# Random-feature attention and a feed-forward in one kernel: feed-forward chunks of 512 tokens with one PSUM bank for h, and float64 weights decoded by VectorE and ScalarE in slices of 1024 columns

## The chip, the cores and the metric

The kernel runs on one core of a Trainium2 chip. The metric is the time on the device in microseconds (us), the median of several runs. TensorE does the matrix products (PE in the profile; PEld is its loading of the stationary operand), VectorE is DVE, ScalarE is ACT, GpSimd is POOL, SyncE is SP and issues the DMAs. Products land in PSUM, which has eight banks of 512 float32 columns on 128 partitions.

## What is computed

Attention with positive random features, then a feed-forward with g(h) = h - tanh(h), on 8 batches of 576 tokens, 8 heads of 64 columns, 128 features, d_model 512 and d_ff 2048:

```python
def phi(x):                      # x: q or k, times 64 ** -0.25
    proj = np.einsum('bhsd,md->bhsm', x, omega)
    h = proj - np.sum(x * x, axis=-1, keepdims=True) / 2.0
    return np.exp(h - np.max(h, axis=-1, keepdims=True)) / np.sqrt(m)
kv = np.einsum('bhsm,bhsd->bhmd', phi(k), v)
num = np.einsum('bhsm,bhmd->bhsd', phi(q), kv)
den = np.einsum('bhsm,bhm->bhs', phi(q), np.sum(phi(k), axis=2))[..., None] + 1e-06
x = (num / den)                  # as [4608 tokens, 512]
h = x @ w_in                     # [4608, 2048]
out = (h - np.tanh(h)) @ w_out   # [4608, 512]
```

q, k, v and omega are float32. The two weight matrices arrive as float64; the kernel gets their 8-byte words.

## The kernel before, in words

**Precision.** A product of float32 operands is made of three fast products: each operand is split into hi (rounded to the format float32r) and lo (the rest), and hi*hi, hi*lo and lo*hi are added up in PSUM. So every operand costs a cast (hi, mostly ScalarE) and a subtraction (lo, mostly VectorE).

**Attention** is cut into units, each a Python generator whose `yield`s separate stages. `k_unit(b, c)` makes kv and the sums z of one batch and one pair of heads; `q_unit(ch, c, ...)` makes 128 rows of x (one pair of heads) for a chunk of 256 tokens: features (L128 to L136, or L146 to L150 in float32), denominators (L322, L325), normalisation (L327 to L331), four transposes into a bank `pt` (L338), the product with kv into a bank `pn` (L346, or L362 and L363), and x. In the "native" mode of the start, units work in float32 directly; later ones use split operands (`k_single`). A unit of queries writes its part of xh and xl itself (L372, L373). `tick` moves every open unit forward by one stage and opens the new ones that a table `start` names for this tick.

**Feed-forward.** Chunks have 256 tokens (TC), 18 in all. For a chunk, a step takes two 128-row slices of d_ff: `ffn_h` (L421) makes h of both side by side in one bank of PSUM, 2 x 12 matmuls of 256 columns, then g = tanh(h) on ScalarE (L432), g = h - g on VectorE (L433), gh (L434, ScalarE) and gl (L435, VectorE or, for the first two chunks, GpSimd). `ffn_out` (L438) adds 12 matmuls of 512 columns to two output banks. The products of a step follow one step after its h. Two banks, h0 and h1, alternate for h. The other banks are po0 and po1 (outputs), pj0 and pj1 (projections), pk, and pt. `ffn_store` (L449) copies an output bank to SBUF and stores it.

**Weights.** `decode` (L384) turns float64 words into hi and lo, 512 or 256 columns at a time: ScalarE scales the upper words (L398), GpSimd scales them back (L399), VectorE shifts, masks and merges them (L400, L402, L405) and multiplies the lower mantissa bits in (L406), ScalarE rounds to hi (L408), GpSimd subtracts (L409), and GpSimd or VectorE adds up lo (L410).

**Order of work.** First batch 0's keys and the queries of chunks 0 and 1 in float32. Then eight steps, in each of which two slices of the weights are decoded and chunks 0 and 1 take their step with them, beside keys of batch 1 and queries of chunks 2 and 3. Then chunk after chunk, with one tick of attention behind each `ffn_h` and each `ffn_out`. The program text is not the order on the chip: `schedule_with_timeline_sim=True` has the tile framework lay out each engine's instructions at build time by its own estimate of when each is ready, with program order as the priority. After that each engine takes its list strictly in order.

Of the kernel before, what the change touches and what calls it, by code (L numbers as in the profile page):

```python
# [22 lines left out]
NS = NF // 2          # steps of the feed-forward: two slices each  # L23
# [8 lines left out]
def favor_attention_ffn(ctx: ExitStack, tc: tile.TileContext, qT, kT, va, vb, vt, omT, w_in, w_out, out):  # L32
# [12 lines left out]
    # SBUF: from the left the constants, the working tiles and the weights, as they are decoded;  # L45
    # from the right the tiles of the attention and the scratch of the decoding.
# [12 lines left out]
    # What differs between the start and the rest: buffers, PSUM banks and engines.  # L59
# [26 lines left out]
    omf = sb.tile([P, DM], F32, tag="o", name="omf")[:, 0:M]  # L86
# [5 lines left out]
    ones = const.tile([P, P], F32R, name="ones")  # L92
    nc.scalar.activation(ones, ident, AF.Copy, bias=1.0, scale=0.0)
    om2 = om.rearrange("p a m -> p (a m)")
    aq = open_pool("aq")
    kv0 = open_pool("kv0")
    # both heads' at once for tokens in float32, with -SCALE
    om_bd = kv0.tile([P, 2, M], F32, name="om_bd")
# [24 lines left out]
        # om hi and om lo side by side in one pass, added on the way out  # L123
# [15 lines left out]
    def features_f(f, toks, name):  # L139
        """The same for tokens of both heads as float32 in one pass: [tile, head]."""  # L140
# [12 lines left out]
    kvf = {}   # batch: [kv | 0] and [0 | kv] of each head pair, in float32  # L153
    kvs = {}   # (batch, head pair): [kv hi | lo] of both heads, z on every partition

    def k_unit(b, c):
        """kv and z of the heads 2c and 2c + 1 of batch b, a stage at a time."""
        n = f"{b}_{c}"
        f = att("kf", [P, S], F32, f"kf_{n}")
        nc.sync.dma_start(f, kT[c, :, b * S : (b + 1) * S])  # L160
# [4 lines left out]
        nc.sync.dma_start(v[:, 0:4, 0:D], va[b, c, 0])  # L165
        nc.sync.dma_start(v[:, 6:10, 0:D], va[b, c, 1])
        nc.sync.dma_start(v[0:D, 4:6, 0:D], vb[b, c])
# [16 lines left out]
        # head 0 as columns [hi | lo], head 1 as [lo | hi]  # L184
# [17 lines left out]
    def k_single(b, c, f):  # L202
        """The same by single-pass products: [v hi | v lo]^T [k hi | k lo], whose four parts add up
        to kv^T. z is ones^T times the sum of the tiles of k."""
        n = f"{b}_{c}"
        v = att("vr", [P, 9, D], F32, f"v_{n}")
        nc.sync.dma_start(v, vt[b - 2, c])
        yield
# [5 lines left out]
        pk = ps.tile([P, 2, 2, M], F32, tag=bank("pk"), name=f"pk_{n}")  # L214
        zs = att("zs", [P, 2, M], F32, f"zs_{n}")

        def split(ph, t, n_t):
            """k and v of n_t tiles from t on as [hi | lo], by pairs."""
            ku = []
            for g in range(0, n_t, 2):  # L220
# [7 lines left out]
                else:   # the tile of both heads, kept apart by zeros  # L228
# [22 lines left out]
        ku = split(pa, 0, 4)  # L251
        zsum(pa, 0)
        yield
        pm = features(tiles[4:5], f"km{n}")
        kv(0, ku, True, False)
# [22 lines left out]
        for i in range(2):  # L278
            nc.tensor.matmul(pk[:, 1].rearrange("p h m -> p (h m)"), ones,  # L279
                             zhl[:, i].rearrange("p h m -> p (h m)"), start=i == 0, stop=i == 1)  # L280
        kvt = att("kvs", [P, 2, D], F32, f"kvs_{n}")
# [9 lines left out]
    def q_unit(ch, c, x_out):  # L291
        """The rows of x of the heads 2c and 2c + 1 for chunk ch, a stage at a time."""
        n = f"{ch}_{c}"
        t0 = ch * TC
        pieces = []   # of the chunk, by batch
        t = t0
        while t < t0 + TC:
            e = min((t // S + 1) * S, t0 + TC)
            pieces.append((t // S, t - t0, e - t0))
            t = e  # L300
        f = att("qf", [P, TC], F32, f"qf_{n}")
        native = mode["native"]
        nc.sync.dma_start(f, qT[c, :, t0 : t0 + TC])
# [4 lines left out]
        else:  # L308
            x = att("qx", [P, 2, TC], F32R, f"qx_{n}")
# [26 lines left out]
        pt = ps.tile([P, 2 * TC], F32, tag=bank("pt"), name=f"pt_{n}")  # L336
        for i in range(4):
            nc.tensor.transpose(pt[:, i * P : (i + 1) * P], ph[:, ix(i // 2, i % 2)], ident)  # L338
        if native and all(b in kvf for b, s, e in pieces):
            qf = att("qh", [P, 2, TC], F32, f"qt_{n}")  # L340
            nc.scalar.copy(qf.rearrange("p h t -> p (h t)"), pt)
            yield
            pn = ps.tile([P, TC], F32, tag=bank("pt"), name=f"pn_{n}")
# [8 lines left out]
        qh = att("qh", [P, 2, TC], F32R, f"qh_{n}")  # L352
        ql = att("ql", [P, 2, TC], F32R, f"ql_{n}")
# [4 lines left out]
        pn = ps.tile([P, 2, TC], F32, tag=bank("pt"), name=f"pn_{n}")  # L358
# [5 lines left out]
        tmp = att("tmp", [P, TC], F32, f"tmp_{n}")  # L364
        xs = sb.tile([P, TC], F32, tag="xs", name=f"xs_{n}", bufs=2)
# [4 lines left out]
        yield  # L370
        xh, xl = x_out(ch)
        nc.scalar.copy(xh[:, c], xs)  # L372
        mode["lo"].tensor_sub(xl[:, c], xs, xh[:, c].bitcast(F32))  # L373
        xdone[ch] = xdone.get(ch, 0) + 1

# [181 lines left out]
    while gens:  # L557
        tick()
# [81 lines left out]
```

## Time and profile before

| | |
|---|---|
| median of 3 runs | 1107.13 us (1106.38 to 1108.35) |
| profiled execution, first to last instruction | 1105.4 us |
| instructions | 21115 |
| mean granted TensorE clock | 0.986 |
| DMA | 55.94 MB, mean 51 GB/s |

In the profile, a row of a group gives line, engine, operation, the tiles written and read, the shape and count; then total busy time and the mean duration in ns; then the idle time of the engine just before, with what ended it. A row of the timeline gives start and duration in us from the span's start. PEclk is the share of its full clock that TensorE was granted. Matmuls are pipelined, so their durations overlap and only the distance of their starts is a price.

### The profile page before, as it was taken

To read this page: it belongs to the slowest core of one execution; us is meant where nothing else is said; L and a number is where in the kernel's file an instruction comes from. 1 tells how busy PE (TensorE), PEld (TensorE's weight loads), DVE (VectorE), ACT (ScalarE), POOL (GpSimd) and SP (SyncE) were. 2 spreads that over 40 slices of the span, in tenths; PEclk is the share of its full clock that TensorE was granted. 3 is DMA by queue.
4 is the path that set the end of the run, shared out by engine and by line. 5 is a ranking of instruction groups with operands and counts; after the bars stand their busy time and mean duration, and the time that the engine had idled before them with its cause. 6 is when DMAs were issued, how large, how long until landed. Compare 5 with 4: busy or idle time off the path is not lost. (4 is left out here: it accounts for less than half of the span.)

```text
span 1105.4 us, 21115 instructions
## 1 busy us (share of the span) xinstructions
PE 1063.0 (96%) x6968; PEld 966.1 (87%) x6968; DVE 900.0 (81%) x3079; ACT 703.7 (64%) x1850; POOL 403.1 (36%) x659
## 2 busy tenths in 40 slices
PE   9797888799999999999999999999999999999998
PEld 7577677689989999999999999899999999999997
DVE  5989999989999888678888888998888888666522
ACT  6654445577677776567776776677777766556421
POOL 2787677635553331023333333343333333000000
PEclk9989889999999999999999999999999999999999
DMA  8233312221111111101111111111111110000000
GB/s 232 95 117 99 117 65 96 65 69 31 60 32 51 32 51 32 34 11 51 32 51 29 51 32 51 32 52 32 52 32 51 32 36 15 30 10 25 1 20 20
DMA packets 39244, 55.94 MB, mean 51 GB/s; under 512 B 12896, under 2 KB 22240, under 8 KB 39136
## 3 DMA queue, kind: packets, MB, share of 16 engines
q1 hardware_dynamic: 39056, 54.57, 15.9%
q8 instruction: 55, 0.90, 0.3%
q14 instruction: 53, 0.43, 0.1%
q10 hardware_dynamic: 80, 0.03, 0.0%
HBM read 45.15 MB, written 9.44 MB: 49 GB/s over the span
## 5 line engine op out<-in xcount | busy, mean ns | idle before, releaser
L428 PE MATMUL h<-xh,wih 128*128 128x256 f32 x1152 | 331.0, 288 | 7.7 <-DVE g L433 7.5
L428 PE MATMUL h<-xh,wil 128*128 128x256 f32 x1152 | 329.9, 287 | 2.2 <-DVE wil L410 1.9
L428 PE MATMUL h<-xl,wih 128*128 128x256 f32 x1152 | 329.9, 286 | 0.0
L428 PEld LDWEIGHTS h<-xh,wih 128*128 128x128 f32 x1152 | 221.0, 192 | 14.9 <-issue 5.5
L428 PEld LDWEIGHTS h<-xl,wih 128*128 128x128 f32 x1152 | 221.3, 192 | 4.6 <-issue 0.8
L428 PEld LDWEIGHTS h<-xh,wil 128*128 128x128 f32 x1152 | 221.2, 192 | 3.5 <-DVE wil L410 2.4
L445 PE MATMUL po<-woh,gh 128*128 128x512 f32 x544 | 214.2, 394 | 0.0
L446 PE MATMUL po<-wol,gh 128*128 128x512 f32 x544 | 214.0, 393 | 0.0
L447 PE MATMUL po<-woh,gl 128*128 128x512 f32 x544 | 211.9, 391 | 0.0
L433 DVE TENSOR_TENSOR g<-h,g 128x512 f32<-128x512 f32 x144 | 98.8, 686 | 59.8 <-ACT g L432 58.9
L434 ACT CAST gh<-g 128x512 fp32r<-128x512 f32 x144 | 89.4, 621 | 86.0 <-DVE g L433 83.0
L432 ACT ACTIVATE g<-h 128x512 f32<-128x512 f32 x144 | 85.2, 592 | 87.6 <-PE h L428 79.2
L435 DVE TENSOR_TENSOR gl<-g,gh 128x512 fp32r<-128x512 f32 x128 | 99.7, 779 | 37.8 <-ACT gh L434 36.2
L447 PEld LDWEIGHTS po<-woh,gl 128*128 128x128 f32 x544 | 102.3, 188 | 21.0 <-DVE gl L435 0.4
L445 PEld LDWEIGHTS po<-woh,gh 128*128 128x128 f32 x544 | 102.7, 189 | 16.2
L446 PEld LDWEIGHTS po<-wol,gh 128*128 128x128 f32 x544 | 102.7, 189 | 14.9
L322 DVE CUSTOM_DVE_ANT_0 junk<-phi_q,zb 128x128 f32<-128x128 f32 (+1 forms) x320 | 101.8, 321 | 13.8 <-ACT zb L285 0.4
L225 POOL TENSOR_TENSOR khl<-phi_ka,khl 128x256 fp32r<-128x256 f32 x48 | 38.2, 801 | 116.9 <-DVE khl L224 109.8
L136 ACT ACTIVATE phi_q<-phi_q,nb_q 128x128 f32<-128x128 f32 x232 | 75.7, 391 | 2.5 <-DVE nb_q L132 2.2
L233 POOL CAST vhl<-v 128x128 fp32r<-128x128 f32 (+1 forms) x144 | 45.2, 315 | 85.2 <-PE pk L241 73.8
L356 DVE TENSOR_TENSOR ql<-pt,qh 128x512 fp32r<-128x512 f32 x64 | 43.9, 686 | 29.6 <-ACT qh L355 29.3
L338 PE MATMUL pt<-ident,phi_q 128*128 128x128 f32 x288 | 50.0, 279 | 11.2 <-DVE xs L369 3.8
(152 smaller groups left out, 2198.6 us busy)
## 6 DMA issues: line engine op xcount, KB each, us to landing
kf<-kT SPq DMA_DIRECT2D x32, 288.0 KB, 2.9
qf<-qT SPq DMA_DIRECT2D x72, 128.0 KB, 2.1
out<-o SPq DMA_DIRECT2D x36, 256.0 KB, 2.0
v<-vt SPq DMA_DIRECT2D x24, 288.0 KB, 2.8
raw_i<-w_in SPq DMA_DIRECT2D x12, 512.0 KB, 3.9
raw_o<-w_out SPq DMA_DIRECT2D x12, 512.0 KB, 3.3
v<-va SPq DMA_DIRECT2D x16, 128.0 KB, 3.6
raw_i<-w_in SPq DMA_DIRECT2D x8, 256.0 KB, 2.8
```

Of the source, the lines that this page charges most:

```text
L136: nc.scalar.activation(ph[:, j], ph[:, j], AF.Exp, bias=nb[:, j : j + 1], scale=-1.0)
L233: nc.gpsimd.tensor_copy(u[p, i, 0], v[p, j])
L322: nc.vector.tensor_tensor_reduce(bank("junk")[r], ph[r, i], kvs[b, c][1][r, h], scale=1.0, scalar=EPS, op0=ALU.mult, op1=ALU.add, accum_ou ...
L338: nc.tensor.transpose(pt[:, i * P : (i + 1) * P], ph[:, ix(i // 2, i % 2)], ident)
L428: nc.tensor.matmul(p[:, j], w, x, start=i == 0, stop=i == len(prods) - 1)
L432: nc.scalar.activation(g, p, AF.Tanh)
L433: nc.vector.tensor_sub(g, p, g)
L434: nc.scalar.copy(gh, g)
L435: mode["gl"].tensor_sub(gl, g, gh.bitcast(F32))
L445: nc.tensor.matmul(po[t], h, woh[f], start=first, stop=False)
L446: nc.tensor.matmul(po[t], h, wol[f], start=False, stop=False)
L447: nc.tensor.matmul(po[t], l, woh[f], start=False, stop=last)
```

## The change

- `TC` becomes 512, with 9 chunks; units of queries keep 256 tokens (`TQ`). A step of the feed-forward is one slice of d_ff: 12 matmuls of 512 columns for h, 12 for the outputs.
- h has a single bank, `h`. Four banks hold the outputs (po0 to po3), one is pk, and two, a0 and a1, take turns for projections, transposes and `pn`.
- x is written as float32 by the query units and split for a whole chunk by `split_x`, into single buffers. Finished outputs are copied into those x tiles, by ScalarE and VectorE in turn, and stored from there.
- In `ffn_out` the products with gl come after all others of the step, except in the last slice.
- A slice of w_in and one of w_out lie together, 1024 columns, fetched by one DMA (`fetch`) and decoded by nine passes, three on ScalarE and six on VectorE; GpSimd has none. There are two raw buffers and one each of the working tiles a and m.
- The weights are decoded beside one first chunk (512 tokens), a slice per step, with the keys of batch 1, half of batch 2's, and the queries of the next 512 tokens, all in float32. In this phase the loads of SyncE's queue are kept in program order (`load`).
- Of the first eight units' normalisations VectorE takes half; in the first chunk ScalarE takes all. gl is always VectorE's.

```diff
-TC = 256              # tokens of a chunk
+TC = 512
+TQ = 256
+NW0 = 10
...
+    def load(dst, src):
+        i = nc.sync.dma_start(dst, src)
+        if mode.get("chain"):
+            tc.keep_in_program_order(i)
...
-            xh, xl = x_out(ch)
-            nc.scalar.copy(xh[:, c], pn)
-            nc.vector.tensor_sub(xl[:, c], pn, xh[:, c].bitcast(F32))
+            nc.scalar.copy(x_out(ch, c), pn)
...
+    def fetch(f):
+        raws[f] = dec.tile([P, 2 * DM], U64, tag="raw", name=f"raw{f}", bufs=2)
+        load(raws[f], w[f])
...
+    def decode(f):
...
+        a = dec.tile([P, 2 * DM], U32, tag="a", name=f"a{f}", bufs=1)
+        m = dec.tile([P, 2 * DM], U32, tag="m", name=f"m{f}", bufs=1)
+        p = raws[f].bitcast(U32)[:, 0 : 2 * DM]
+        nc.scalar.activation(m, mid, AF.Copy, scale=128.0)
+        nc.scalar.activation(a.bitcast(F32), topf, AF.Abs)
+        nc.vector.tensor_scalar(a.bitcast(F32), a.bitcast(F32), 2.0**-15, 122879.9921875,
+                                op0=ALU.max, op1=ALU.min)
+        nc.vector.tensor_scalar(a, a, 3, 0x3FFFF000, op0=ALU.logical_shift_left, op1=ALU.bitwise_and)
+        nc.vector.scalar_tensor_tensor(out=a, in0=top, scalar=0xC0000000, in1=a,
                                        op0=ALU.bitwise_and, op1=ALU.bitwise_or)
+        nc.scalar.copy(hi, a.bitcast(F32))
+        nc.vector.scalar_tensor_tensor(out=m, in0=top, scalar=23, in1=m,
+                                       op0=ALU.logical_shift_left, op1=ALU.bitwise_or)
+        nc.vector.tensor_scalar(p, a, 0xFF800000, None, op0=ALU.bitwise_and)
+        nc.vector.scalar_tensor_tensor(out=lo, in0=m, scalar=2.0**-43, in1=p.bitcast(F32),
                                        op0=ALU.mult, op1=ALU.mult)
...
+    def split_x(n):
+        xhs[n] = []
+        for c in range(NC):
+            xh, xl = [sb.tile([P, TC], F32R, tag=f"x{k}{c}", name=f"x{k}{c}_{n}") for k in "hl"]
+            nc.scalar.copy(xh, xfs[n][c])
+            nc.vector.tensor_sub(xl, xfs[n][c], xh.bitcast(F32))
+            xhs[n].append((xh, xl))
...
+    def ffn_h(n, s):
+        p = ps.tile([P, TC], F32, tag="h", name=f"h_{n}_{s}")
+        prods = [(wt[s][:, i, c * P : (c + 1) * P], xhs[n][c][j]) for c in range(NC)
+                 for i, j in ((0, 0), (0, 1), (1, 0))]
...
+    def run(n, s):
+        prev = state["prev"]
+        def beat():
+            tick(start.pop(state["t"], ()))
+            state["t"] += 1
+        def h():
+            if s == 0:
+                while sum(xdone.get(n * TC // TQ + i, 0) for i in range(TC // TQ)) < NC * TC // TQ:
+                    tick((), True)
+                split_x(n)
+            state["prev"] = (n, s, *ffn_h(n, s))
+        h()
+        beat()
+        if prev is not None:
+            ffn_out(*prev)
+            if s == 0:
+                ffn_store(n - 1)
+        beat()
...
+    ab = ["a0", "a1"]
+    mode.update(pj=ab, pk=["pk"], pt=ab, norm=[nc.scalar], kvw=(sb, 6), zb=(sb, 6))
...
+    for s in range(NF):
+        if len(wt) == NW0 and not start and not gens:
             close_pool("a0")
+            weight_tiles(open_pool("w1", "left"), range(NW0, NF))
+        decode(s)
+        if fetched < NF:
+            fetch(fetched)
+            fetched += 1
+        run(0, s)
```

More of the change, by code (lines that the diff above doesn't have):

```diff
@@ L369, in q_unit @@
         nc.vector.tensor_add(xs[D:P], pn[D:P, 1], tmp[D:P])
[L370 to L373, printed above, removed]
         xdone[ch] = xdone.get(ch, 0) + 1
-    wih, wil, woh, wol = {}, {}, {}, {}
+    wt = {}
     def weight_tiles(pool, fs):
         for f in fs:
-            for name, d in (("wih", wih), ("wil", wil), ("woh", woh), ("wol", wol)):
-                d[f] = pool.tile([P, DM], F32R, name=f"{name}{f}")
@@ L412, in decode_slice @@
[L412 to L431 removed]
+            wt[f] = pool.tile([P, 2, 2 * DM], F32R, name=f"w{f}")
@@ L434, in ffn_h @@
         nc.scalar.copy(gh, g)
-        mode["gl"].tensor_sub(gl, g, gh.bitcast(F32))
+        nc.vector.tensor_sub(gl, g, gh.bitcast(F32))
         return gh, gl
-    def ffn_out(s, gh, gl, po):
-        for t in range(TC // P):
-            for j in range(2):
-                f = 2 * s + j
-                h = gh[:, j, t * P : (t + 1) * P]
-                l = gl[:, j, t * P : (t + 1) * P]
-                first, last = f == 0, f == NF - 1
-                nc.tensor.matmul(po[t], h, woh[f], start=first, stop=False)
-                nc.tensor.matmul(po[t], h, wol[f], start=False, stop=False)
-                nc.tensor.matmul(po[t], l, woh[f], start=False, stop=last)
@@ L463, in out_tiles, with ffn_out @@
-    def out_tiles(ch, tags=("po0", "po1")):
-        return [ps.tile([P, DM], F32, tag=t, name=f"{t}_{ch}") for t in tags]
-    need = {b: (b * S) // TC for b in range(B)}
-    x_of = {}
+    po = {}
+    def ffn_out(n, s, gh, gl):
+        if s == 0:
+            po[n] = [ps.tile([P, DM], F32, tag=f"po{t}", name=f"po{t}_{n}") for t in range(TC // P)]
+        first, last = s == 0, s == NF - 1
+        tok = [slice(t * P, (t + 1) * P) for t in range(TC // P)]
+        for t, p in enumerate(po[n]):
+            nc.tensor.matmul(p, gh[:, tok[t]], wt[s][:, 0, DM:], start=first, stop=False)
+            nc.tensor.matmul(p, gh[:, tok[t]], wt[s][:, 1, DM:], start=False, stop=False)
+            if last:
+                nc.tensor.matmul(p, gl[:, tok[t]], wt[s][:, 0, DM:], start=False, stop=True)
+        if not last:
+            for t, p in enumerate(po[n]):
+                nc.tensor.matmul(p, gl[:, tok[t]], wt[s][:, 0, DM:], start=False, stop=False)
@@ new lines, in ffn_store @@
+    def ffn_store(n):
+        for t, p in enumerate(po[n]):
+            o = xfs[min(n + 1, NCH - 1)][t]
+            r = n * TC + t * P
+            if n == NCH - 1 and t == TC // P - 1:
+                for e, h in ((nc.vector, slice(0, DM // 2)), (nc.scalar, slice(DM // 2, DM))):
+                    copy(e, o[:, h], p[:, h])
+                    nc.sync.dma_start(out[r : r + P, h], o[:, h])
+            else:
+                copy((nc.scalar, nc.vector)[t % 2], o, p)
+                nc.sync.dma_start(out[r : r + P, :], o)
@@ L469, in favor_attention_ffn @@
+    need = {b: (b * S) // TQ for b in range(B)}
+    xfs, xhs = {}, {}
     xdone = {}
@@ L601, in favor_attention_ffn @@
-    ffn_out(*prev)
-    ffn_store(NCH - 1, prev[-1])
+            start.setdefault(16 * (need[b] - 4) - 17 + 6 * c, []).append(("k", b, c))
+    start = {t0 + k: v for k, v in start.items()}
+    for n in range(1, NCH):
+        for s in range(NF):
+            run(n, s)
+    ffn_out(*state["prev"])
+    ffn_store(NCH - 1)
     for name in list(pools)[::-1]:
```

265 lines of the change are left out of this document (85 added, 180 removed).

## The prediction

> **What bounds the kernel now.** I read the page's first part, then the busy time by stretch, then single matmuls in the timeline.
>
> ```profile
> PE 1063.0 (96%) x6968; PEld 966.1 (87%) x6968; DVE 900.0 (81%) x3079; ACT 703.7 (64%) x1850; POOL 403.1 (36%) x659
> ```
>
> ```profile
> core 0 of [0], span 1105.4 us
> core 0: us, PE busy (x) PEld busy (x) DVE busy (x) ACT busy (x) POOL busy (x), PEclk, DMA share, GB/s
> 0.00:215.00 215.00, 178.76 (x980) 149.68 (x980) 193.71 (x399) 115.34 (x304) 147.70 (x175) 0.93 0.35 111
> 215.00:400.00 185.00, 183.15 (x1245) 168.55 (x1246) 166.34 (x618) 136.18 (x363) 80.32 (x147) 1.00 0.16 48
> 400.00:1000.00 600.00, 599.38 (x4093) 555.43 (x4092) 496.62 (x1941) 413.73 (x1103) 175.08 (x338) 1.00 0.12 36
> 1000.00:1105.00 105.00, 101.66 (x654) 92.40 (x653) 43.32 (x124) 38.47 (x82) 0.00 (x0) 1.00 0.04 16
> ```
>
> The reader should see two kernels in one. From 215 us on TensorE has work at all times (599.38 of 600 us), so there only cheaper matmuls, or waits put between them, move the end. In the first 215 us TensorE lacks 36 us and runs at 0.93 of its clock, while VectorE is 90% busy: there the decoding of the weights sets the pace. The change touches both.
>
> **Part 1: 512 tokens per matmul of h.** Counts are from the code: h has 18 chunks x 16 slices x 12 = 3456 matmuls of 256 columns now, and 9 x 16 x 12 = 1728 of 512 afterwards. The products for the output stay 1728 of 512. Near the end no attention is mixed in, and the pitch can be read off:
>
> ```profile
> 1051.05 0.40 PE L445 MATMUL po<-woh,gh 128*128 128x512 f32 x1
> ...
> 1053.80 0.28 PE L428 MATMUL h<-xh,wih 128*128 128x256 f32 x1
> ...
> 1056.67 0.40 PE L445 MATMUL po<-woh,gh 128*128 128x512 f32 x1
> ```
>
> Twelve matmuls of 512 columns lie between the first two rows: 2.75 us, 0.229 us each. Twenty-four of 256 lie between the second and third: 2.87 us, 0.1196 us each. (The durations in the rows are longer because matmuls overlap; only starts count.) Today's cost of h is 3456 x 0.1196 = 413.3 us; at the pitch of the output products it becomes 1728 x 0.229 = 395.7 us. Unrounded pitches keep it at 17 to 19 us; I take **-18 us**. Bounds: nothing, if two 256s simply add up to a 512 for these operands (the output products have the activations stationary, h has the weights); on the other side -19, since no row shows a shorter pitch at this width. The nearest row is the same shape on the same engine, so I stay with it.
>
> The Trainium skill (TensorE: Matmul & The Clock Gate, "Wait — 56ns, not 53.3ns?") gives a warm matmul N/2.4 GHz plus about 2.5 ns; this speaks against the gain. By that rule the 1728 matmuls saved are worth an estimated 4 us, not 18. The trace disagrees with the rule in both pitches (119.6 and 229 ns against 109 and 216), so I go by the rows.
>
> **Part 2: the decoding.** Everything VectorE does for it today writes or reads a_i or a_o:
>
> ```profile
> 0.00:215.00 215.00, 61.57 (x84) 11.81 (x20) 34.54 (x36) 0.93 0.35 111
> ```
>
> ```profile
> 0.00:215.00 215.00, 78.09 (x96) 11.62 (x20) 17.73 (x24) 0.93 0.35 111
> ```
>
> The columns are VectorE, ScalarE, GpSimd; VectorE spends 61.57 + 78.09 = 139.7 us. The same operations have very different durations in it:
>
> ```profile
> L402 DVE SCALAR_TENSOR_TENSOR raw_o<-raw_o,a_o x8: 674/1026/1792, 44.6 to 122.1; 128x512 uint32<-128x512 uint32 x8
> ```
>
> ```profile
> L402 DVE SCALAR_TENSOR_TENSOR raw_o<-raw_o,a_o x6: 409/421/430, 178.9 to 211.7; 128x256 uint32<-128x256 uint32 x6
> ```
>
> ```profile
> L400 DVE TENSOR_SCALAR a_i<-a_i x9: 413/1505/1516, 30.9 to 120.6; 128x512 uint32<-128x512 uint32 x9
> ```
>
> ```profile
> L400 DVE TENSOR_SCALAR a_i<-a_i x4: 264/340/527, 186.8 to 203.0; 128x256 uint32<-128x256 uint32 x4
> ```
>
> The figures are minimum/median/maximum in ns. An instruction costs 674 ns undisturbed and up to 1792 with GpSimd at work beside it (147.70 us busy in this stretch). The change takes GpSimd out of the decoding, so I price by minima, extended to 1024 columns: two-input operations 674 + 2 x (674 - 409) = 1204 ns, one-input operations 413 + 2 x (413 - 264) = 711 ns. A slice has three of each: 5.75 us, 16 slices **92 us** (upper bound: today's 139.7). ScalarE gets three passes per slice:
>
> ```profile
> L398 ACT ACTIVATE a_i<-raw_i x9: 662/669/750, 41.2 to 125.9; 128x512 f32<-128x512 f32 x9
> ```
>
> ```profile
> L398 ACT ACTIVATE a_i<-raw_i x4: 429/437/448, 182.6 to 198.4; 128x256 f32<-128x256 f32 x4
> ```
>
> That is 669 + 2 x (669 - 437) = 1133 ns, 54 us in all. Today there are two passes, 11.81 + 11.62 us for one and about as much for the other, so ScalarE gains some 8 us of work; at 115.34 of 215 us busy it has room.
>
> VectorE takes over the residue gl of the first slices, which GpSimd makes now:
>
> ```profile
> L433 DVE TENSOR_TENSOR g<-h,g 128x512 f32<-128x512 f32 x144 | 98.8, 686 | 59.8 <-ACT g L432 58.9
> ...
> L435 DVE TENSOR_TENSOR gl<-g,gh 128x512 fp32r<-128x512 f32 x128 | 99.7, 779 | 37.8 <-ACT gh L434 36.2
> ```
>
> Of 144 residues 128 are VectorE's, so 16 more at about 0.69: 11 us. Half of the 32 normalisations of the first eight query units move to it, at the price it pays later:
>
> ```profile
> L331 DVE TENSOR_SCALAR phi_q<-phi_q,dn 128x128 f32<-128x128 f32 x177 | 47.8, 325 | 1.0
> ```
>
> 16 x 0.325 = 5 us. The start also has more attention in it. Up to 215 us there are now these, one reduction per query unit and three per key unit:
>
> ```profile
> L148 DVE TENSOR_REDUCE nb_k<-pj_k 128x4 f32<-128x512 f32 (+1 forms) x24 | 14.1, 592 | 6.0 <-PE pj_k L146 6.0
> ...
> L148 DVE TENSOR_REDUCE nb_q<-pj_q 128x4 f32<-128x512 f32 x13 | 8.8, 681 | 0.9 <-PE pj_q L146 0.9
> ```
>
> That is 13 query and 8 key units; by the new order of work 16 and 10 are started before the first 512 tokens end. VectorE's attention so far is 193.71 - 139.7 - 10 (g) = 44 us for 21 units, 2.1 each: 5 more are 10.5 us. So VectorE has 193.7 - 139.7 + 92 + 11 + 5 + 10.5 = 172.5 us to do before the first 512 tokens are through; today that point is here, where the first output is copied out:
>
> ```profile
> 220.76 0.58 ACT L456 COPY o<-po 128x512 f32<-128x512 f32 x1
> ```
>
> At today's 90% share 172.5 us take 192 us, at 80% they take 216. I take 85%, 203 us: the start stays short of work as before, and the single buffers of a and m tie ScalarE's pass for slice f+1 to VectorE's last operation of slice f (with ScalarE's pass of 1.1 us exposed on all 16 slices that wait would cost 18 us; other VectorE work covers it). This is 18 us earlier. The five extra units are also off TensorE's later list: about 16 matmuls for a query unit, 23 for a key unit, 3 x 16 + 2 x 23 = 94 at 0.12 us: 11 us. **-29 us** in all; by the two shares -40 and -16, and nothing at all if the share falls to 74%.
>
> The loads stand in SyncE's queue in program order now, so a fetch whose buffer is not free holds back the key and query loads behind it. A slice's 1 MB needs at most two of these:
>
> ```profile
> raw_i<-w_in SPq DMA_DIRECT2D x12, 512.0 KB, 3.9
> ```
>
> 7.8 us against over 10 us per slice on VectorE: hidden, by a buffer that is fetched one slice ahead. If decoding fell under 8 us, this would be next.
>
> **Part 3: what the banks cost.** Four banks go to the outputs, so h has one instead of two: the matmuls of slice s+1 must wait for the tanh and the subtraction of slice s, and TensorE's whole queue stands behind them. Between two blocks of h lie 12 output products (2.75 us) and attention. The trace shows how late the subtraction comes when nothing forces it; these are the first and last cases from 244 us on in which it ends after the next block has begun:
>
> ```profile
> 247.10 0.68 DVE L433 TENSOR_TENSOR g<-h,g 128x512 f32<-128x512 f32 x1
> 247.11 0.28 PE L428 MATMUL h<-xh,wih 128*128 128x256 f32 x1
> ```
>
> ```profile
> 1063.12 0.69 DVE L433 TENSOR_TENSOR g<-h,g 128x512 f32<-128x512 f32 x1 [3.03 <-ACT g L432]
> ...
> 1063.68 0.28 PE L428 MATMUL h<-xh,wih 128*128 128x256 f32 x1
> ```
>
> There are 39 such steps of 124, and they are late by 61 us together. That is the upper bound. But the order on each engine is planned anew: attention matmuls, now mostly inside the block of h, can be moved into the gap. How many there are:
>
> ```profile
> L433 DVE TENSOR_TENSOR g<-h,g 128x512 f32<-128x512 f32 x86 | 59.0, 686 | 18.5 <-ACT g L432 17.9
> ```
>
> This row is for 400 to 1000 us: 600 / 86 = 6.97 us per step, less 5.62 us of feed-forward, 1.35 us of attention. With these the gap is 4.0 us, and only 16 of 124 steps end later than that, by 11 us together. That is the lower bound; I take **+16 us**, nearer to it, because a held TensorE also gives VectorE (83% busy there) time to catch up.
>
> At each of the 8 changes of chunk the four x tiles are split anew, into single buffers, only after the last h of the old chunk: four casts and four subtractions of about 0.7 us. The first pair lets the first three matmuls go, and 2.75 us of output products lie before them, as many more (the last slice's) can be taken forward: 0 to 2 us each, **+5 us**. The projections and transposes share two banks instead of three, and the finished outputs leave from the x tiles. I put both at nothing: TensorE has other matmuls to take while an attention step waits; without that cover each late evacuation would hold it by about 1 us. The end has the same copy and store, halved between two engines: under 0.5 us.
>
> **Sum.** Against the profiled span: 1105.4 - 18 - 29 + 16 + 5 = 1079.4 us. The median of the runs, 1107.13, lies 1.7 us above this span, so **1081 us**.
>
> **The rivals.** *The bank of h becomes the bound (slower).* In the 112 steps with attention beside them the subtraction queues behind attention on VectorE as it does now, and TensorE stands still. For: the 39 late steps, and a VectorE that grows busier. Against: the new order above, and that TensorE now waits for g no longer than this, 7.5 us in 1152 first matmuls of a triple:
>
> ```profile
> L428 PE MATMUL h<-xh,wih 128*128 128x256 f32 x1152 | 331.0, 288 | 7.7 <-DVE g L433 7.5
> ```
>
>  With the full 61 us and 10 us at the chunk changes: 1107.1 - 18 - 29 + 61 + 10 = 1131 us. It decides from 42 us of waits, 0.37 us per step.
>
> *The start gains nothing.* VectorE stays at 74% because decode, attention and feed-forward hand each other work through ScalarE. Then 1107.1 - 18 + 16 + 5 = 1110 us.
>
> *The wider matmul is no cheaper.* Two 256s make one 512 in h: 1081 + 18 = 1099 us. The rule of the Trainium skill in Part 1 would give an estimated 1095.
>
> **How the numbers follow.** Forecast 0.52 (own range 1060 to 1099: the start's two shares, with 11 and 0 us of waits in Part 3, or 16 and 10), h bank 0.21, start 0.13, pitch 0.09, the rest for mixtures. Within 0.2% is about 2.2 us, what a measurement of this kernel can tell from no change. Faster: 0.52 + 0.09, the better part of the start's case and of the mixtures: 0.69; same 0.05; slower 0.26. For 8 in 10 the range reaches from 1060 to 1118: it takes in the other two cases and the bank's up to 48 us of waits.
>
> **What would show it.** Right: starts of h matmuls 0.229 us apart; VectorE instructions of the decode near 0.71 and 1.2 us; the first output copied out near 203 us; waits of h for g of about 16 us in the waits view; a stretch from 400 to 900 us in which TensorE still has work 97% of the time. Wrong: idle TensorE before the first matmul of each h, over 0.37 us on the mean; a first output after 215 us; a pitch near 0.239.

## The result, and the profile after

The changed kernel takes 1337.32 us (median of 4 runs, 1332.91 to 1341.42) against 1107.37 us (4 runs, 1106.38 to 1108.35): a ratio of 1.2077, 95% interval 1.2048 to 1.2105. The forecast was 1081 us and the range ended at 1118. The profiled execution is 1334.4 us long, at a mean granted clock of 0.878 instead of 0.986.

From the page, the busy times and two of its strips of 40 slices (33 us each):

```profile
PE 1170.8 (88%) x5258; PEld 937.7 (70%) x5258; DVE 871.0 (65%) x2925; ACT 725.6 (54%) x1769; POOL 242.8 (18%) x472
...
PE   9699877999789976998699976998699967997898
...
PEclk9799978899869985999589956998589966997799
```

Every engine's share fell, so none of them became the bound: something makes all of them wait, and the strips show a dip about every 4.3 slices, which is the time of one chunk. TensorE's clock dips with its work. Of the 229 us between the two spans, TensorE's idle time makes up 121 (163.6 us instead of 42.4); the other 108 are busy time, although the matmuls were to become cheaper. The busy time by stretch, in the order start, second chunk, one chunk change, the rest of that chunk's attention, end:

```profile
core 0: us, PE busy (x) PEld busy (x) DVE busy (x) ACT busy (x) POOL busy (x), PEclk, DMA share, GB/s
0.00:241.00 241.00, 202.59 (x920) 156.65 (x920) 179.13 (x409) 154.04 (x359) 23.46 (x34) 0.91 0.35 108
241.00:346.00 105.00, 104.59 (x505) 87.83 (x506) 70.48 (x257) 59.17 (x144) 21.82 (x41) 0.97 0.11 31
776.00:818.00 42.00, 25.10 (x81) 17.95 (x81) 29.30 (x129) 24.05 (x66) 9.90 (x20) 0.50 0.14 43
829.00:914.00 85.00, 85.00 (x421) 71.66 (x420) 58.28 (x200) 47.31 (x118) 23.73 (x50) 1.00 0.07 20
1210.00:1334.00 124.00, 105.44 (x433) 82.66 (x431) 40.97 (x105) 35.12 (x71) 0.00 (x0) 0.89 0.05 19
```

Inside a chunk TensorE is full (85.00 of 85 us). At the change of chunk it does 81 matmuls in 42 us, at half its clock. TensorE's timeline at that change, with the first row of each group of three h matmuls and the waits in brackets (idle time before, and what ended it):

```profile
776.34 0.63 PE L435 MATMUL h<-xh,w 128*128 128x512 f32 x1
...
788.88 0.77 PE L136 MATMUL pj_q<-om,qx 128*128 128x256 f32 x2 [0.92 <-DVE x L375]
789.44 0.79 PE L435 MATMUL h<-xh,w 128*128 128x512 f32 x1
...
794.35 1.12 PE L346 MATMUL pt<-ident,phi_q 128*128 128x128 f32 x4 [1.95 <-DVE phi_q L339]
...
806.10 0.77 PE L136 MATMUL pj_q<-om,qx 128*128 128x256 f32 x2 [3.50 <-DVE x L375]
806.66 0.79 PE L435 MATMUL h<-xh,w 128*128 128x512 f32 x1
...
810.79 1.08 PE L346 MATMUL pt<-ident,phi_q 128*128 128x128 f32 x4 [2.20 <-DVE phi_q L339]
...
817.48 0.79 PE L435 MATMUL h<-xh,w 128*128 128x512 f32 x1
```

The 12 matmuls of the chunk's first h need four x tiles, and the last query units of the chunk, one for each tile, are still on their way. They come one behind the other: the projections (pj_q) of a unit wait until L375 has read the `pn` of the unit before out of the bank, then its transposes wait for its normalisation, and only after its x come the next three matmuls of h. What should have been 2.75 us takes 41 us. With the clock at a half, an h matmul lasts 0.63 to 0.80 us there, instead of 0.39 inside the chunk; how much of the 108 us the clock makes up was not separated.

Where the 229 us between the two spans come from, by the starts of the first h matmul of each chunk of 512 tokens (for the kernel before, of each second chunk):

| | before | after | difference |
|---|---|---|---|
| start, up to the second 512 tokens | 216.3 us | 241.4 us | +25 |
| each of the next seven times 512 tokens, mean | 112.5 us | 138.4 us | 7 x 25.9 = +181 |
| last 512 tokens, to the end | 101.6 us | 123.9 us | +22 |

### The profile page after: what moved, and what is told of

Read it like the earlier page. It is cut to its first block, busy times and chain, and to the rows that moved or that the text cites. A ratio compares the mean times of both kernels' runs of the same rounds, so it can differ in the third digit from the quotient of the medians.

```text
span 1334.4 us, 17184 instructions
## 1 busy us (share of the span) xinstructions
PE 1170.8 (88%) x5258; PEld 937.7 (70%) x5258; DVE 871.0 (65%) x2925; ACT 725.6 (54%) x1769; POOL 242.8 (18%) x472
## 4 chain that ended last, share of the span: by engine, by line
PE 70%; DVE 14%; ACT 9%; issue 3%; DMA 2%; POOL 1%; SPq 0%; DVEq 0%; ACTq 0%; POOLq 0%
PE h L435 29%; PE po L453 9%; PE po L454 9%; PE po L459 8%; PE pt L346 3%; PE pn L369 2%; DVE junk L330 2%; PE pk L247 2%; PE pj_q L136 2%; PE pn L368 2%; DMA raw<-w 1%; DVE ql L362 1%; PE pk L187 1%; PE pj_k L154 1%; DVE x L375 1%
## 5 line engine op out<-in xcount | busy, mean ns | idle before, releaser
L435 PE MATMUL h<-xh,w 128*128 128x512 f32 x1152 | 419.4, 422 | 24.5 <-DVE g L440 17.2
L435 PEld LDWEIGHTS h<-xh,w 128*128 128x128 f32 x1152 | 231.5, 201 | 77.4 <-DVE g L440 20.8
L435 PE MATMUL h<-xl,w 128*128 128x512 f32 x576 | 242.4, 421 | 0.4 <-DVE xl L427 0.2
L453 PE MATMUL po<-w,gh 128*128 128x512 f32 x576 | 227.7, 395 | 2.1 <-ACT gh L441 2.1
L454 PE MATMUL po<-w,gh 128*128 128x512 f32 x576 | 226.1, 393 | 0.0
L459 PE MATMUL po<-w,gl 128*128 128x512 f32 x540 | 156.7, 394 | 0.0
L435 PEld LDWEIGHTS h<-xl,w 128*128 128x128 f32 x576 | 116.0, 201 | 30.0 <-DVE xl L427 9.8
L453 PEld LDWEIGHTS po<-w,gh 128*128 128x128 f32 x576 | 109.3, 190 | 25.2 <-ACT gh L441 3.0
L454 PEld LDWEIGHTS po<-w,gh 128*128 128x128 f32 x576 | 109.1, 189 | 21.1
L459 PEld LDWEIGHTS po<-w,gl 128*128 128x128 f32 x540 | 96.8, 188 | 16.5 <-DVE raw L416 0.4
L136 PE MATMUL pj_q<-om,qx 128*128 128x256 f32 x224 | 56.6, 341 | 32.9 <-DVE x L375 31.4
L136 PEld LDWEIGHTS pj_q<-om,qx 128*128 128x128 f32 x224 | 44.8, 229 | 42.8 <-ACT phi_q L137 17.1
```

The source lines that it names most:

```text
L136: nc.tensor.matmul(pj[:, i], lhs[g + i], om2, start=True, stop=True)
L435: nc.tensor.matmul(p, w_, x, start=i == 0, stop=i == len(prods) - 1)
L453: nc.tensor.matmul(p, gh[:, tok[t]], wt[s][:, 0, DM:], start=first, stop=False)
L454: nc.tensor.matmul(p, gh[:, tok[t]], wt[s][:, 1, DM:], start=False, stop=False)
L459: nc.tensor.matmul(p, gl[:, tok[t]], wt[s][:, 0, DM:], start=False, stop=False)
```

## The experiments

Four theories stood against each other. **T1**: projections, transposes and `pn` share two banks in fixed turn, in place of three, so query units pass one behind the other, the feed-forward runs ahead of them and stands at the chunk change. **T2**: the single bank of h. **T3**: the single SBUF buffers of the units (qf, qx, tmp) make their chain long. **T4**: in the start, loads kept in program order delay the weights. "Order" is the variant of T1 in which TensorE's list, not the banks, does the harm.

A third bank cannot simply be given to the changed kernel, whose eight banks are all in use. In the first two runs, and in all later ones of the changed kernel with a third bank, the outputs of the third and fourth token tile are therefore summed in one bank: their separation is left out, the number of matmuls is not changed. Each time below is from a single run unless a ratio stands with it; the four runs of the changed kernel lie 8.5 us apart.

**A third bank for attention** (the bank freed takes pt and pn from the second chunk on):

```diff
-        po[n] = [ps.tile(..., tag=f"po{t}") for t in range(TC // P)]
+        po[n] = [ps.tile(..., tag=f"po{t}") for t in range(TC // P - 1)]
+        po[n].append(po[n][-1])
...
+        pj=["a0", "a1"], pt=["po3"],
```

> The products of the last two token tiles of a chunk go to one output bank (so these two tiles' outputs are not kept apart and the output is not the reference's; the number and shape of all matmuls stay), and the bank set free serves the transposes and kv products of the query units from the second chunk on, beside the two banks of the projections, as before the change. Theory 1, the attention's units go one after another because projections, transposes and kv products share two banks in turn: the distance of query units beside the feed-forward falls from 20 to 26 us to about 14 us, the waits of 30 to 43 us at each change of chunk fall under 5 us, and the time falls from 1337 to about 1130 us (1090 to 1170). Theory 2, the single bank of h holds TensorE: no change, above 1310 us. Theory 3, the units are slow by their single buffers in SBUF or by their own chain beside wide matmuls: above 1290 us.

Measured: 1159.66 us, clock 0.960, so 178 us less, of which 90 are idle time of TensorE and 87 busy time. The total came as expected, the chunk changes did not: from the third to the eighth chunk the twelve matmuls of the first h, 2.5 us long in the last chunk, still lie over 8 to 18 us (31 to 42 with two banks), and the waits were to fall under 5. The buffers were not touched, so T3 alone does not explain the 178 us. The kernel before, from its third chunk on, also has one buffer each of qx, qh, ql and tmp, and two of qf. It has two of each split x tile, the changed kernel one; more buffers were not run.

**The same bank for h instead.**

```diff
+        tag="h" if s % 2 == 0 or n == 0 else "po3"
```

> The same bank is set free in the same way (outputs of the last two token tiles not kept apart), but it is given to h as a second bank, in turn with the first, from the second chunk on. Theory 2, the single bank of h holds TensorE: the time falls to 1200 us or less. Theories 1 and 3: within 25 us of 1337 us, with the same waits of 30 to 43 us at the changes of chunk.

Measured: 1339.73 us. T2 falls. The outputs share a bank here too, so that was not what helped in the run before.

**Two banks, but one for each kind.**

```diff
+        pj=["a0"], pt=["a1"],
```

> From the second chunk on projections have bank a0 to themselves and transposes and kv products bank a1; no bank is added. Theory 1: the next unit's projections no longer wait for the x of the unit before, but two pairs of tiles now share one projection bank; the time falls to 1180 to 1270 us. Theories 2 and 3: within 25 us of 1337 us, or slower.

Measured: 1316.07 us, 21 less. T1 had expected far more: the fixed turn, one half of that theory, is not the main harm.

**Loads free of program order.**

```diff
-        chain=True, kvw=(a0, 4),
+        chain=False, kvw=(a0, 4),
```

> The loads of the first chunk are no longer kept in program order, all else as after the change. Theory 4, the fetches of the weights stand behind key and query loads whose buffers are not free: the fetches of slices 7 to 12, now up to 29 us apart, come 10 us apart or less, the last slice is decoded by about 205 us instead of 234, and the time falls by 20 to 35 us to about 1308 us. If VectorE's own work sets the pace of the decoding: the last slice is decoded at 225 us or later and the time stays within 10 us of 1337.

Measured: 1330.57 us, a miss in size: 7 us, no more than runs of the changed kernel differ by, of which 5 are in the start (the second chunk begins at 236 us). The last slice is decoded at 227 us, as for the rival, but not by its cause (see "The start").

The pace of attention can be counted. L375 (L369 in the kernel before) runs once for each query unit; these are its rows between 400 and 1000 us, of the kernel before, after, and after with a third bank:

```profile
L369 DVE TENSOR_TENSOR xs<-pn,tmp x44: 427/428/430, 403.9 to 999.5; 64x256 f32<-64x256 f32 x44
```

```profile
L375 DVE TENSOR_TENSOR x<-pn,tmp x33: 427/428/429, 412.4 to 985.8; 64x256 f32<-64x256 f32 x33
```

```profile
L375 DVE TENSOR_TENSOR x<-pn,tmp x42: 427/427/429, 403.6 to 999.1; 64x256 f32<-64x256 f32 x42
```

44 units in 596 us before, one per 13.9 us; 33 in 573 us after, one per 17.9; 42 with the third bank, one per 14.5. Since every 512 tokens take eight units, their pace and the time of a chunk are one and the same; that the banks set it is shown by the runs that change the banks alone. TensorE's waits in the two versions of the changed kernel (total, times, longest), first with two banks, then with three:

```profile
PE pj_q L136 <- DVE x L375: 31.4, 19, 3.8
PE pt L346 <- DVE phi_q L339: 28.7, 22, 2.9
PE h L435 <- DVE g L440: 17.2, 9, 4.9
```

```profile
PE h L435 <- DVE g L440: 16.1, 8, 4.9
PE pt L346 <- ACT phi_q L337: 5.2, 5, 2.9
```

Both of the units' waits go with the third bank (pt for phi_q of VectorE falls to 1.8 us; the 5.2 us for ScalarE's were 5.1 with two banks), and that of h for g, the bank I had feared, is nearly the same.

**Order or banks.** In the changed kernel, at the changes to its sixth, seventh and eighth chunk, about 102 of a chunk's some 203 attention matmuls stand in TensorE's list between the start of the last step of one chunk and the start of the second step of the next: half of them in two of sixteen steps. In the kernel before it is mostly 18 to 34 of some 95, about what two of eight steps would hold if they were spread evenly. So the next runs keep TensorE's list in program order, in which it is 16 to 23 of some 200 at most changes, on two banks and on three:

```diff
+            i = nc.tensor.matmul(*a, **k)      # and transpose
+            if mode.get("order"):              # True from the second chunk on
+                tc.keep_in_program_order(i)
```

> Changed kernel with its two shared banks as they are; from the second chunk on, TensorE's queue keeps its products in the order in which the beats name them, so the attention's products stand evenly among the steps instead of half of them (some 103 of 204 for a chunk) around the chunk change. Theory A (the bunching in TensorE's queue costs the time; the banks themselves stand empty more than half of the time, held for 253 of 600 bank-us between 700 and 1000): chunk changes shrink to under 8 us each, total 1120 to 1200, about 1150. Rival B (two banks in fixed turn make a unit's chain too long whatever the queue's order): TensorE waits inside the steps instead, for pj, pt or pn, and the total stays at 1270 or more.

> The same order of TensorE's queue, and the outputs of the third and fourth token tile of a chunk summed in one bank (left out: their separation), the freed bank taking pt and pn from the second chunk on. Against 1160 with the freed bank alone: theory A gives 1100 to 1150, since 39 of 200 products still stood at a chunk change there; rival B gives less than 1160 only if order and bank both count; if in-order products wait for their inputs inside each step (single buffers, chain of the unit), 1180 or more.

Measured: 1300.61 us on two banks, 1154.84 on three (the theory of the order had expected 1120 to 1200 and 1100 to 1150: both missed). The units pass at this pace with two banks and the even list:

```profile
L388 DVE TENSOR_TENSOR x<-pn,tmp x35: 427/427/428, 405.1 to 995.6; 64x256 f32<-64x256 f32 x35
```

and this is what TensorE does with it:

```profile
770.00:790.00 20.00, 15.92 (x73) 12.87 (x72) 13.82 (x50) 9.36 (x26) 5.45 (x8) 0.91 0.14 36
790.00:810.00 20.00, 17.76 (x89) 14.67 (x87) 13.50 (x38) 12.42 (x26) 0.00 (x0) 1.00 0.12 42
810.00:830.00 20.00, 17.11 (x85) 14.35 (x86) 15.12 (x59) 12.14 (x31) 6.11 (x14) 1.00 0.14 41
830.00:850.00 20.00, 16.41 (x89) 13.61 (x88) 15.77 (x60) 12.54 (x35) 8.22 (x18) 1.00 0.07 22
```

The standstill at the chunk change is spread over all steps (TensorE 80 to 89% busy in each stretch), and the total is nearly as bad. The theory of the order falls: it decides where the time is lost, and 37 us of it; the number of banks decides the rest.

**The banks alone, on the kernel before**, with its chunks of 256, its decode and its output banks; each run has one of the last four lines in place of the first:

```diff
-    mode.update(pj=["pj0", "pj1"], pk=["pk"], pt=["pt"])
+    ab = ["pj0", "pt"]
+    mode.update(pj=ab, pk=["pk"], pt=ab)                       # two in turn
+    mode.update(pj=["pj0", "pj1"], pk=["pk"], pt=["pt"], h=["h0"])  # one for h
+    mode.update(pj=ab, pk=["pk"], pt=ab, h=["h0"])             # both
+    mode.update(pj=["pj0"], pk=["pk"], pt=["pt"])              # two, no turn
```

> Kernel before with its chunks of 256, its old decode and two banks for h; from the third chunk on, the projections and the transposes share two banks in fixed turn (pj0 and pt; pj1 lies idle), as in the changed kernel. Theory (two banks in turn make the query units pass one after another): the units' distance goes from 13.8 us to 16 to 20 us, total 1180 to 1380. Rival (sharing hurts only beside chunks of 512, whose wide products and single x tiles make the chunk change wait): 1107 to 1130.

> Kernel before with one bank for h from the third chunk on, all else as it was. If one h bank costs little, as the run with a second h bank on the changed kernel says: 1107 to 1130. If the h bank counts at this chunk size: over 1150, by the time from the end of an h product to the end of g, some 2 us on 128 steps.

> Kernel before with both: two shared banks for projections and transposes and one bank for h from the third chunk on, chunks of 256 and the old decode kept. If the banks alone make the changed kernel slow, 1200 or more; if the chunk of 512 is needed for it, 1110 to 1150.

> Kernel before with one bank for projections and one for transposes from the third chunk on, nothing shared (pj1 lies idle): two banks, but no turn between the kinds. If the fixed turn between the kinds is what lengthens a unit: 1110 to 1160 against 1248 with the two shared. If the number of banks is: 1200 to 1280, as on the changed kernel, where this split gave only 21 us.

Measured: two banks in turn 1247.92 us, one bank for h 1115.53, both 1226.05, two banks without a turn 1258.63; the kernel before on the same chips 1107.21 to 1107.5. Waits of TensorE and units with two banks in turn, on the kernel before:

```profile
PE pj_km L128 <- DVE dn L325: 19.7, 8, 2.9
PE pt L338 <- DVE phi_q L331: 16.0, 22, 3.2
PE pj_q L128 <- DVE xs L369: 14.4, 14, 1.5
```

```profile
L369 DVE TENSOR_TENSOR xs<-pn,tmp x37: 427/427/428, 404.8 to 999.6; 64x256 f32<-64x256 f32 x37
```

One edit of the bank list, with nothing else of the change, costs 140 us. The same waits of pj_q and pt appear, at chunks of 256 tokens, besides one of key units (pj_km). With one bank for each kind and no turn the time is no better, so of T1 the number of banks stays and the turn falls. The single bank of h costs 8 us here, and on top of the two banks nothing (22 us less, which no run explains).

**The start.** It was to become 18 of Part 2's 29 us shorter and became 25 longer.

```diff
-    mode.update(pj=ab, pk=["pk"], pt=ab, norm=[nc.scalar], ...)
+    mode.update(pj=ab, pk=["pk"], pt=["po3"], norm=[nc.scalar], ...)   # third bank in the start, with free loads
...
-            weight_tiles(open_pool("w1", "left"), range(NW0, NF))
+            wt.update({f: wt[f - NW0] for f in range(NW0, NF)})        # place
```

> The freed bank of the earlier run (outputs of the third and fourth token tile in one bank; left out: their separation) takes pt and pn from the first chunk on, and all loads are free of program order. Reading: the place of weight slices 10 to 15 comes free only when the start's attention units have ended, at about 190 us, and these units pass one after another through the two banks. If so: they end by about 165, the second chunk begins by 215 instead of 241 to 243, total 1125 to 1145 against 1160. Rival: VectorE's work or something else than banks sets the units' pace in the start; the second chunk begins at 235 or later, total 1148 to 1162.

> The changed kernel with loads free of program order, and weight slices 10 to 15 decoded into the tiles of slices 0 to 5 (left out: their own tiles, so later chunks use these weights for both), so that no slice waits for the place of the start's attention. Against 1331 us with free loads alone, whose second chunk began at 236 us. If the place sets the start: all slices decoded by 165 us, the second chunk begins at 195 to 210, total 1290 to 1310. Rival (decode and units share VectorE and ScalarE, their pace sets the start): second chunk at 225 or later, total 1320 to 1335.

> The same two tiles in one on top of the kernel with the freed bank from the start on and free loads (1143 us, second chunk at 231 us; left out besides: the outputs of the third and fourth token tile are summed in one bank). If the place sets the start: second chunk at 185 to 205, total 1105 to 1125. Rival: second chunk at 220 or later, total 1135 to 1145.

Measured: 1143.01 us with the third bank in the start as well (second chunk at 231 us, so a miss on the start, though the total is in its range; the third bank and the free loads together gave 17 us); 1311.05 us with the place free (20 us less than free loads alone); 1125.73 us with both (17 less; second chunk at 193 us). The last two totals lie about 1 us above their expected ranges. Slices 9 and 10 of the weights, with the loads free but the place as in the change, VectorE's last operation on each:

```profile
111.97 1.23 DVE L417 SCALAR_TENSOR_TENSOR w<-m,raw 128x1024 fp32r<-128x1024 uint32 x1
...
191.50 1.23 DVE L417 SCALAR_TENSOR_TENSOR w<-m,raw 128x1024 fp32r<-128x1024 uint32 x1
```

They lie 79.5 us apart, where 7 to 12 are usual, because the tiles of slices 10 to 15 take the place of the pool in which the start's attention works, and its last units, in the same run, finish here:

```profile
L375 DVE TENSOR_TENSOR x<-pn,tmp x2: 427/427/427, 187.6 to 191.1; 64x256 f32<-64x256 f32 x2
```

With the place free (first row, all 16 slices) the decode no longer stops, but the x tiles of the second chunk are split only when the units are done (second row):

```profile
L417 DVE SCALAR_TENSOR_TENSOR w<-m,raw x16: 1186/1218/1228, 31.6 to 167.9; 128x1024 fp32r<-128x1024 uint32 x16
```

```profile
L427 DVE TENSOR_TENSOR xl<-x,xh x4: 692/692/693, 178.5 to 217.0; 128x512 fp32r<-128x512 f32 x4
```

The second chunk's first matmul comes at 184 us (expected: 195 to 210), its last x tile at 217. So the place held the weights back, and behind it the units are late: two causes in a row, of which only the first was undone. The order of the loads stands in the same row: in the changed kernel itself slices 7, 8 and 9 each come 18 to 32 us behind the one before, with free loads 8 to 10, and then the place takes up what was won.

**The new decode alone**, in the kernel before, its tiling, banks and pieces of 512 and 256 columns kept, in a single run and then in six:

```diff
-        a = mode["dec"].tile([P, n], U32, tag="a", name=f"a_{name}", bufs=mode["ndec"])
-        nc.scalar.activation(af, topf, AF.Copy, scale=2.0**111)
-        nc.gpsimd.tensor_scalar(af, af, 2.0**-112, 2.0**-111, op0=ALU.mult, op1=ALU.mult)
...
+        a = mode["dec"].tile([P, n], U32, tag="a", name=f"a_{name}", bufs=mode["ndec"] - 1)
+        m = mode["dec"].tile([P, n], U32, tag="m", name=f"m_{name}", bufs=1)
+        nc.scalar.activation(m, mid, AF.Copy, scale=128.0)
+        nc.scalar.activation(a.bitcast(F32), topf, AF.Abs)
...
```

> Kernel before, with chunks of 256 and its banks, its buffers of the decode one fewer; only its decode is replaced by the changed kernel's sequence on VectorE and ScalarE, in the old slices of 512 and 256 columns. VectorE's share of the decode falls from about 137 us to about 92 us by the two traces, in a stretch (20 to 240 us) in which it was 94% busy. If VectorE sets the start there: 1070 to 1085. Rival, the start's attention units and ScalarE set it: 1095 to 1110.

> The kernel before with the new decode alone, timed in rounds: 1100 in one look against 1108, so 0.990 to 0.996 of the time before.

Measured: 1100.49 us in the single run (1070 to 1085 if VectorE set the start there: a miss; the rival's 1095 to 1110 holds), then 1098.40 us against 1107.50, ratio 0.9933, interval 0.9915 to 0.9951. From 20 to 200 us, the kernel before and then this one:

```profile
20.00:200.00 180.00, 149.71 (x822) 126.08 (x820) 172.51 (x349) 96.25 (x245) 134.77 (x143) 0.91 0.32 104
```

```profile
20.00:200.00 180.00, 154.10 (x874) 131.19 (x873) 158.18 (x448) 119.08 (x304) 46.14 (x56) 0.93 0.34 107
```

VectorE has room now (158.18 of 180 us instead of 172.51), TensorE little more work in it: VectorE alone did not set the start. This version is 0.7% faster than the kernel before, clear of the spread of its runs.

## Why the prediction was wrong, step by step

- **The step that failed** is a half sentence of Part 3: "The projections and transposes share two banks instead of three ... I put both at nothing: TensorE has other matmuls to take while an attention step waits". The third bank is worth 178 us on the changed kernel and its loss 140 us on the kernel before. The cover exists inside a chunk, where TensorE was full, but it is borrowed: the feed-forward that TensorE takes meanwhile belongs to a chunk that is already complete, and it runs out at the chunk change, where the next one needs the units that waited. From 400 to 900 us TensorE had work 89% of the time, not 97. The text's own price without cover, "each late evacuation would hold it by about 1 us", was never multiplied by the number of units, and no rival had it. Measured, TensorE waited 19 times for the x of the unit before and 22 times for the normalisation, 60 us in all, and the half clock came on top. Seen as a pace, eight query units per 512 tokens at 17.9 us are 143 us, while the kernel before does 512 tokens in 112.5 us; the 17.9 is known from the result alone.
- **Chunk changes, +5 us.** Wrong for the same reason: the four casts and subtractions were costed, not the wait for x. With the third bank the change that begins at 718 us still takes some 8 us instead of 41, and the other chunks from the third to the eighth 10 to 18.
- **Part 1, -18 us.** Right at full clock. In the last chunk, h and output products lie 2.72 us per twelve, 0.227 us each, a little under the 0.229 of the forecast:

```profile
1290.97 0.39 PE L453 MATMUL po<-w,gh 128*128 128x512 f32 x1
...
1293.69 0.39 PE L435 MATMUL h<-xh,w 128*128 128x512 f32 x1
...
1296.41 0.39 PE L453 MATMUL po<-w,gh 128*128 128x512 f32 x1
```

- **Part 2, durations.** Right: VectorE's operations of the decode, at 0.711 and 1.204 us in the forecast, and ScalarE's, at 1.133:

```profile
L414 DVE SCALAR_TENSOR_TENSOR m<-raw,m 128x1024 uint32<-128x1024 uint32 x16 | 19.6, 1228 | 8.0 <-ACT m L402 7.9
...
L407 DVE TENSOR_SCALAR a<-a 128x1024 f32<-128x1024 f32 x16 | 11.0, 686 | 1.5 <-ACT a L406 1.5
```

```profile
L402 ACT ACTIVATE m<-raw 128x1024 uint32<-128x1024 uint16 x16 | 18.4, 1151 | 7.2 <-DMA raw<-w 5.4 <-DVE w L417 1.7
```

- **Part 2, the start, -29 us.** Wrong. VectorE's work came out near the sum (179.13 us up to 241 us, forecast 172.5), its share did not: 179.13 / 241 is 74%, not 85, and the first output is copied out at 250 us, not 203. At 74% the text had put the gain at nothing, and named that as a rival; the share came true, but the runs put the loads and the place ahead of its reason (work handed on through ScalarE), which no run tested. "Hidden, by a buffer that is fetched one slice ahead" failed (slices 7 to 9 came 18 to 32 us apart, though free loads alone gave only 7 us), and the place of slices 10 to 15, which the code shows, was not in the sum at all (20 us).
- **Part 3, the bank of h, +16 us.** Near in size, by luck: 17.2 us of waits for g, against 7.5 before, and +8 us on the kernel before with one bank. But the waits stand elsewhere than forecast. Two of the nine (8.1 us) are in the start and at the second chunk's first h; the other seven, 0.9 to 2.1 us each, come at the second h of a chunk, and the steps inside a chunk have none. (The gap of 4.0 us is 4.1 by its own terms, 2.75 + 1.35, which changes nothing.) The rival built on it (1131 us) was the wrong one to fear.

The Trainium skill (Perfetto Trace Analysis, "Matmuls") says that independent groups of matmuls should rotate through different banks so that emptying one overlaps the products of the next. The trace agrees, with 178 us for one bank of three; the forecast had not weighed it.

Open: with the third bank 512 tokens still take 117.2 us, 4.7 more than before, in spite of cheaper h matmuls. The drawn-out first h of its chunks would account for more than that, but the run with three banks and program order has none of it (2.5 us each) and is only 5 us faster, so what holds the third bank's version back is not known. Two banks cost more with chunks of 512 (1337 us) than of 256 (1248); the start accounts for 25 us of these 89, and the rest was not split up. Giving the transposes the bank pk, which the key units use, was not run.

## What to carry to other kernels

When banks or buffers are taken from a side chain of work, price the chain as a pace: the time per unit it will have against the time per unit that the main work needs, and treat "other work covers the wait" as a loan that falls due where the main work next needs the chain. Before a large rearrangement, a cheap test is one edit of the old kernel's bank list, which here showed 140 us with nothing else changed. Where new tiles take over the place of a pool, the last user of that pool belongs to the sum of the stage.

## What the runs showed of the hardware that was not expected

TensorE's granted clock fell to a half at a chunk change although no long gap stands before the fall. Five-microsecond windows of the changed kernel, and the timeline's rows around TensorE's longest idle time in the second of them:

```profile
765.00:770.00 5.00, 5.00 (x28) 4.20 (x27) 4.48 (x17) 4.00 (x10) 1.19 (x2) 1.00 0.13 23
770.00:775.00 5.00, 3.50 (x21) 2.76 (x19) 3.26 (x9) 2.06 (x5) 3.96 (x8) 0.82 0.31 97
775.00:780.00 5.00, 3.59 (x10) 2.40 (x10) 4.64 (x27) 4.82 (x15) 0.00 (x0) 0.50 0.15 53
```

```profile
769.73 0.60 PE L346 MATMUL pt<-ident,phi_q 128*128 128x128 f32 x4
771.44 0.51 PE L247 MATMUL pk<-khl,vhl 128*128 128x256 f32 x2 [1.11 <-POOL khl L231]
```

A mean of 0.82 between 1.00 and 0.50 puts the fall at about 773.2 us, some 3 us after the end of the first row (770.33). From there it stayed at 0.50 for some 50 us, with h matmuls of 0.63 to 0.80 us instead of 0.39, and then returned to 1.00. With the list in program order and two banks TensorE had as little work in single windows and kept its clock:

```profile
845.00:850.00 5.00, 3.27 (x19) 2.71 (x18) 3.46 (x15) 2.96 (x8) 1.40 (x4) 1.00 0.00 0
```

The windows on both sides of it are full there. In the same run the clock did fall where a window held 1.11 us of work (780 to 785 us, clock 0.91). The Trainium skill (TensorE: Matmul & The Clock Gate, "HAM oscillation — how this bites in real kernels") warns of idle gaps of more than about 3.4 us; here the clock was down after some 3 us with no gap over 1.11 us, in a window with TensorE 70% busy.
